# Local attention with channel mix: scores moved behind the attention products, transposes one key block earlier, and a strict order on TensorE

## The chip, the core and the metric

The kernel runs on one core of one Trainium2 chip. The metric is the time of one execution on the device in microseconds (us). A core has five engines that matter here, each with its own instruction queue: TensorE (PE in the profile; its weight loads are listed as PEld), VectorE (DVE), ScalarE (ACT), GpSimd (POOL) and SyncE (SP), which issues the transfers between the chip's memory and the core.

## The reference

Two layers are computed one after the other in float32. The first is attention in chunks of 32 queries, each of which sees the 16 keys to its left, its own 32, 8 to its right and 8 memory keys (64 in all). The second is a channel mix over the 512 joined features, with a hidden width of 1024:

```python
# B, H, S, D = 4, 8, 768, 64; chunk, left, right, n_mem = 32, 16, 8, 8
scores = scale * np.matmul(q_c, k_full.transpose(0, 1, 3, 2))
scores = scores - np.max(scores, axis=-1, keepdims=True)
a = np.exp(scores)
a = a / (np.sum(a, axis=-1, keepdims=True) + 1e-09)
out[:, :, c_start:c_end] = np.matmul(a, v_full)
...
x = np.ascontiguousarray(attn_out.transpose(0, 2, 1, 3)).reshape(B, S, H * D)
x_prev = np.concatenate([np.zeros((B, 1, D), dtype=np.float32), x[:, :-1, :]], axis=1)
xk = mu_k * x + (1.0 - mu_k) * x_prev
xr = mu_r * x + (1.0 - mu_r) * x_prev
k = np.maximum(xk @ w_k, 0.0)
v = k * k @ w_v
r = 1.0 / (1.0 + np.exp(-(xr @ w_r)))
return (r * v).astype(np.float32)
```

## The kernel before

**Units.** The 4 x 768 tokens are cut into 12 units of 256 tokens (NU, UTOK), each of two query tiles of 128 tokens; a batch element has three units. Unit u owns the query tiles 2u and 2u+1. What runs for a unit, in the names that the code and the profile use:

- *Scores* (`scores`, f_s, L429; tile s in PSUM): 128 small matmuls of q with its window of keys, on array tiles of 64 rows by 32 columns. Then the softmax: maximum (L442) and subtraction (L447) on VectorE, exp on ScalarE (L453), sum and reciprocal (L457 to L459) and the normalising product (L463) on VectorE, all in one tile e, of which there is a single buffer, as there is of s.
- *Transposes* (`attention`, f_t, L509; tile pt): eight per unit, four for each query tile, each 128x128. Four copies bring them to SBUF (f_bd; recorded in the helper `copy` at L271 on ScalarE and L273 on VectorE; tile aTz).
- *Attention products* (f_a, L526; tile px): 64 matmuls of aTz with the window of V, on array tiles of 128 rows by 64 columns. Copies bring them to xT (f_x), the channel mix's input.
- *Mixing* (`prep`): difference to the token before (L607), the two mixes (L617), and each split into a high part (xh, L271 or L273) and a low part (xl, L633), since TensorE's matmuls here work on such parts, three matmuls for each product.
- *Gates* (`channel_mix`, f_gate, L951; tile pr): two blocks "g" of 24 matmuls, then the sigmoid on ScalarE (L963; tile sg).
- *Key blocks* "h" (f_s1, L1028; tile ph): four blocks of 24 matmuls, each followed by relu (L1047) and square (L1054, L1056), giving kf.
- *Second projection*: units 0 and 1 do it directly ("v", L1112 and L1124; tile pv). From unit 2 on (FAST = 2) `products` does it with seven products of half-size operands instead of eight. Their operands are sums and differences of quarters of kf (L779, L784), split into high (ah, L271 or L273) and low parts (al, L801). Product n is a block "p" of 12 matmuls (L856) onto one of three PSUM tiles: 1 and 2 onto accx, 7 and 4 onto accz, 6, 5 and 3 onto accy. Between two products on the same PSUM tile VectorE must have read it: f_a0 (a copy), L895 and L898 (additions into the output tile o). At the end come the gate products (L916, L926, L928) and the stores (L901). accx and accz share their two PSUM buffers (tag "tp") with pt and px.

**What sets the order.** The program is a plan. Every step is an operation with an engine or a choice of engines, a cost, dependencies, the buffers it takes and uses, and a due time. `te_order` writes TensorE's order down as a list: LEAD for the start, then a loop over the units. From its list it gives each TensorE operation a due time. For a unit from 3 to 9 the list before is

    h0 h1 | t t (unit u+1) | h2 | a a (unit u+1) | h3 | p1 p7 | s (unit u+2) | g g (unit u+1) | p6 p4 p5 p2 p3

where t are the transposes, a the attention products and s the scores. In unit 10 the transposes stand behind h0 already; there and in unit 11 one of the last unit's two gates fills the middle, and no scores are left (s exists up to unit 11, and stands in the list of unit 9). In unit 11, product 2 is written as two halves with product 3 between them.

`Plan.order` runs the planner three times (TURNS), each with due times from the turn before. In a turn, `Plan.turn` always takes the operation that can start earliest by the model of costs, waits and free buffers (`place`), with later due times as a small handicap (EASE). For TensorE only the first operation of the list is looked at while fewer than STRICT operations are placed, that is in strict order; after that any of the next LOOK = 400 may be taken, so that TensorE need not keep the list:

```python
for o in q[: 1 if e == "pe" and len(done) < STRICT else LOOK]:
```

The engines then execute their own queues in the planned order, with semaphores for the dependencies. An engine waits at the head of its queue; nothing behind overtakes.

Of the kernel before, what the change touches and what calls it, by code (L numbers as in the profile page):

```python
# [25 lines left out]
FT = DFF // P  # L26
# [1 line left out]
NEG = -3.0e38  # L28
TINY = 2.0**-112
LOOK = 400  # L30
STRICT = 230
EASE = 0.1
TURNS = 3
LEAD = "s0.0 s0.1 t0 a0 t1 a1 h0.0.0 h0.0.1 s1.0 h0.1.0 h0.2.0 s1.1 h0.3.0 h0.3.1 h0.3.2 h0.3.3 g0.0 g0.1 t2 t3 v0.0.0 a2 a3 v0.0.1 s2.0 v0.1.0 v0.1.1 h1.0 h1.1 t4 t5 h1.2 a4 a5 h1.3 g1.0 g1.1"
# [1 line left out]
FAST = 2  # L36
# [44 lines left out]
class Plan:  # L81
# [7 lines left out]
    def op(self, alts, fn, deps=(), new=(), use=(), due=1e9):  # L89
        fixed = isinstance(alts, tuple)  # L90
        if fixed:
            alts = [alts]
        o = Op([(a + (False,))[:3] for a in alts], fn, deps, new, use, due)
        o.seq, o.fixed = len(self.ops), fixed
        self.ops.append(o)
        return o
# [53 lines left out]
    def turn(self, goal, ease):  # L150
# [9 lines left out]
        while len(done) < len(self.ops):  # L160
            best = None
            for e, q in todo.items():
                for o in q[: 1 if e == "pe" and len(done) < STRICT else LOOK]:
                    p = self.place(o, free, held)
# [21 lines left out]
def te_order():  # L186

    nu = B * S // UTOK
    seq = [tuple([x[0]] + [int(n) for n in x[1:].split(".")]) for x in LEAD.split()]
    for u in range(1, nu):  # L190
        a, b = 2 * u + 2, 2 * u + 3
        g = [("g", u + 1, c) for c in range(QPU)]
        h = [("h", u, f) for f in range(FT // 2)]
        v = [("v", u, c, n) for c in range(QPU) for n in range(2)]
        n = 1 if u == nu - 2 else 2
        seq += h[:n] + [("t", a), ("t", b)] + h[n : n + 1] + [("a", a), ("a", b)] + h[n + 1 :]
        if u >= FAST:
            v = [("p", u, n) for n in (1, 7, 6, 4, 5, 2, 3)]
            if u >= nu - 2:
                g = [("g", nu - 1, u - (nu - 2))]  # L200
            if u == nu - 1:
                v = v[:5] + [("p", u, 2, 0), ("p", u, 3), ("p", u, 2, 1)]
            seq += v[:2] + [("s", u + 2, 0)] + g + v[2:]
            continue
        seq += v[:1] + [("s", u + 2, 0)] + g + v[1:]
    seq = list(dict.fromkeys(seq))
    last = {"t": B * NQT, "a": B * NQT}
    seq = [x for x in seq if x[1] < last.get(x[0], nu)]
    due, t = {}, 6.0
    for x in seq:  # L210
        assert x not in due
        due[x] = t
        t += PE_COST[x[0]] * (0.66 if x[:3] == ("h", 0, 0) else 0.33 if x[:3] == ("h", 0, KT - 1) else 1.32 if x[:2] == ("h", 0) else 1.32 if x[1] == 0 and x[0] in "gv" else 1)
    return due
# [3 lines left out]
def local_attention__then__channel_mix(  # L218
# [60 lines left out]
    units = [(b, u * UTOK) for b in range(B) for u in range(S // UTOK)]  # L279
    NU = len(units)  # L280
    due = te_order()
    chunks = [(w_k, wk_hl, k) for k in range(KT)]
    chunks += [(w_r, wr_hl, k) for k in range(KT // 2)]
# [93 lines left out]
    def wdeps(hl, ks):  # L377
        return [o for k in ks for o in wdone[id(hl[0]), k]]
# [364 lines left out]
    def products(u, ks, o_g, sgs):  # L743
# [3 lines left out]
        b, t0 = units[u]  # L747
# [98 lines left out]
        def f_p(n, cs):  # L846
            def go():
                name, slot = banks[n]
                if n in fresh:
                    T["acc", u, name] = ps(slot.tag, f"acc{name}{u}")  # L850
                o = pairs(T["acc", u, name][:, : DM // 2])
                for c in cs:
                    xh, xl = T["ah", u, n][:, c], low(n)[:, c]
                    wh, wl = weight_of(n, c)
                    for i, (x, w) in enumerate(((xh, wh), (xh, wl), (xl, wh))):
                        nc.tensor.matmul(  # L856
                            o, x, w, start=(n in fresh and c + i == 0), stop=(c == cs[-1] and i == 2), skip_group_check=True
                        )

            return go  # L860

        def prod(n, deps, cs=range(FT // 2), key=()):
            if n in (1, 2, 3):
                wd = wdeps(wv_hl, [0, 1] if n == 1 else [2, 3])
            else:
                wd = turned[n]
            slot = banks[n][1]
            p[n] = op(
                ("pe", 1.36 * len(cs) / 4), f_p(n, list(cs)), list(parts[n]) + wd + deps,
                new=[slot] if n in fresh else [],  # L870
                use=[hs[n], ls[n][0]] + turn_use + ([] if n in fresh else [slot]),
                due=due[("p", u, n) + key],
            )
            return p[n]
# [44 lines left out]
        if last:  # L919
            p2 = prod(2, [p1, a0], range(FT // 4), (0,))  # L920
            p3 = prod(3, [p5, c22])
            p2 = prod(2, [p2], range(FT // 4, FT // 2), (1,))
        else:
            p2 = prod(2, [p1, a0])
            p3 = prod(3, [p5, c22])
# [9 lines left out]
    def channel_mix(u):  # L935
# [160 lines left out]
        if u >= FAST:  # L1096
            products(u, ks, o_g, sgs)
            return
# [75 lines left out]
    with tc.manual_schedule():  # L1174
        for o in plan.order():
            if o.eng == "pe":
                n = 0 if ("ph", 0, 0) in T else int((o.start - busy - 0.2) / (0.43 if busy else 0.86))
# [56 lines left out]
```

## Time and profile before

| | |
|---|---|
| median of 3 runs | 388.85 us (388.57 to 389.3) |
| the profiled execution | 388.38 us |
| span of its instructions | 386.6 us |
| mean granted TensorE clock | 1.000 |
| bytes moved | 48.98 MB, 127 GB/s on average |
| VectorE busy | 317.6 us, 508 instructions |
| ScalarE busy | 220.4 us, 327 instructions |
| a unit in the steady part (units 3 to 8) | 29.97 us |

The span runs from the first to the last instruction; what remains up to the execution's time is start and end around it. In the page, busy times are per engine, and the slices are fortieths of the span. The chain of waits follows the work that ended last back to the start and prints it in order of time: start, duration, engine, tile and line, and a count. It puts each piece at the end of the one before, so that its times lie up to some 0.2 us behind the starts that the timeline shows. The timeline prints start, duration, engine, line, operation, tiles (output <- inputs), shapes and count; in brackets stands the idle time before the instruction and what ended it. Matmuls are pipelined: each lasts longer than the distance to the next.

### The profile page before, as it was taken

The numbers are of one execution on the slowest core, as the hardware profiler recorded it, in microseconds if no ns is written. First come the engines' busy times: TensorE is split into PE (matmuls) and PEld (weight loads), VectorE is DVE, ScalarE is ACT, GpSimd is POOL, SyncE is SP. The second block draws the span as 40 slices with busy tenths as digits, with TensorE's granted clock in tenths as the row PEclk, the third lists the DMA queues.
The fourth block names the chain that finished last, engine by engine and source line by source line (L and its number), as shares of the span: only waits on it lengthen the run. The fifth ranks groups of instructions, "written<-read, shape, count | busy, mean of one in ns | idle before, by whom it ended". The sixth has DMA issues, their size and how long they took to land.

```text
span 386.6 us, 10715 instructions
## 1 busy us (share of the span) xinstructions
PE 380.0 (98%) x4768; PEld 350.2 (91%) x4768; DVE 317.6 (82%) x508; ACT 220.4 (57%) x327; POOL 2.8 (1%) x13
## 2 busy tenths in 40 slices
PE   8899999999999999999999999999999999999996
PEld 6786549989999999999999999999999999999996
DVE  3989998998799699699699699789779879969264
ACT  1789975662644565464565466376267256567260
POOL 2000000000000000000000000000000000000000
PEclk9999999999999999999999999999999999999999
DMA  8999881221152052143134134134134130000101
GB/s 317 420 407 409 310 297 55 110 83 42 27 204 84 30 177 100 54 136 142 56 116 159 57 110 164 56 109 166 56 110 164 57 100 12 30 29 2 54 2 54
DMA packets 13053, 48.98 MB, mean 127 GB/s; under 512 B 1488, under 2 KB 1872, under 8 KB 12496
## 3 DMA queue, kind: packets, MB, share of 16 engines
q1 hardware_dynamic: 13008, 48.31, 33.5%
q8 instruction: 37, 0.61, 0.7%
q14 instruction: 8, 0.07, 0.1%
HBM read 42.01 MB, written 6.29 MB: 125 GB/s over the span
## 4 chain that ended last, share of the span: by engine, by line
PE 96%; DVE 1%; DMA 1%; issue 0%; ACT 0%
PE ph L1028 31%; PE pr L951 15%; PE accy L856 10%; PE accx L856 7%; PE accz L856 7%; PE px L526 6%; PE s L429 4%; PE ph L1000 4%; PE pv L1112 4%; PE pt L509 3%; PE pv L1124 3%; PE pr L943 2%; DMA qk<-in_qk_dram 1%; PE warm L1180 0%; DVE mx L442 0%
## 5 line engine op out<-in xcount | busy, mean ns | idle before, releaser
L1028 PE MATMUL ph<-xh,wk 128*128 128x256 f32 x352 | 99.0, 281 | 0.0
L1028 PE MATMUL ph<-xl,wk 128*128 128x256 f32 x352 | 96.8, 275 | 0.0
L1028 PE MATMUL ph<-xh,wl 128*128 128x256 f32 x352 | 96.8, 275 | 0.0
L1047 ACT ACTIVATE kf<-ph 128x512 f32<-128x512 f32 x47 | 28.0, 597 | 74.4 <-PE ph L1028 74.3
L1028 PEld LDWEIGHTS ph<-xh,wk 128*128 128x128 f32 x352 | 67.5, 192 | 0.9 <-issue 0.2
L1028 PEld LDWEIGHTS ph<-xl,wk 128*128 128x128 f32 x352 | 67.5, 192 | 0.3 <-issue 0.2
L1028 PEld LDWEIGHTS ph<-xh,wl 128*128 128x128 f32 x352 | 67.6, 192 | 0.0
L273 DVE COPY aTz<-pt 64x512 f32<-64x512 f32 x20 | 13.9, 694 | 28.0 <-PE pt L509 18.0
L951 PE MATMUL pr<-wr,xh 128*128 128x512 f32 x88 | 34.3, 390 | 0.0
L801 DVE TENSOR_TENSOR al<-kf,ah 128x512 fp32r<-128x512 f32 x50 | 33.5, 684 | 0.4
L951 PE MATMUL pr<-wl,xh 128*128 128x512 f32 x88 | 33.4, 379 | 0.0
L951 PE MATMUL pr<-wr,xl 128*128 128x512 f32 x88 | 33.4, 379 | 0.0
L453 ACT ACTIVATE e<-e 128x1024 f32<-128x1024 f32 (+1 forms) x13 | 12.9, 992 | 33.6 <-DVE e L447 33.6
L526 PEld LDWEIGHTS px<-aTz,vw 128*64 128x64 f32 x768 | 23.5, 138 | 3.8 <-issue 2.6
L271 ACT CAST ah<-kf 128x512 fp32r<-128x512 f32 x41 | 25.5, 624 | 1.7 <-DVE kf L779 1.1
L526 PE MATMUL px<-aTz,vw 128*64 128x64 f32 x768 | 25.2, 224 | 1.1 <-issue 1.1
L1054 ACT ACTIVATE kf<-kf 128x512 f32<-128x512 f32 x40 | 25.3, 633 | 1.3 <-DVE kf L1049 0.4
L271 ACT CAST xh<-df 128x1024 fp32r<-128x1024 f32 x11 | 16.4, 1493 | 12.2 <-DVE df L617 12.2
L856 PE MATMUL accx<-wv,ah 128*128 128x256 f32 x80 | 22.0, 275 | 0.0
L856 PE MATMUL accx<-wl,ah 128*128 128x256 f32 x80 | 22.0, 275 | 0.0
L856 PE MATMUL accx<-wv,al 128*128 128x256 f32 x80 | 22.0, 275 | 0.0
L963 ACT ACTIVATE sg<-pr 128x512 f32<-128x512 f32 x24 | 14.3, 605 | 9.8 <-PE pr L951 9.8
(124 smaller groups left out, 934.7 us busy)
## 6 DMA issues: line engine op xcount, KB each, us to landing
qk<-in_qk_dram SPq DMA_DIRECT2D x24, 768.0 KB, 6.0
vw<-in_vw_dram SPq DMA_DIRECT2D x24, 512.0 KB, 4.7
out_dram<-o SPq DMA_DIRECT2D x23, 256.0 KB, 2.0
raw<-in_w_k_dram SPq DMA_DIRECT2D x4, 1024.0 KB, 12.0
raw<-in_w_v_dram SPq DMA_DIRECT2D x4, 1024.0 KB, 8.6
raw<-in_w_r_dram SPq DMA_DIRECT2D x2, 1024.0 KB, 8.1
out_dram<-o SPq DMA_DIRECT2D x2, 128.0 KB, 1.7
id_sb<-in_ident_dram SPq DMA_DIRECT2D x1, 64.0 KB, 5.6
```

Source lines behind the costliest of these rows:

```text
L271: e.copy(dst, src)
L429: nc.tensor.matmul(s5[CHUNK * j : CHUNK * (j + 1), h, d - c, r, :], q4[z, r, j, :], k4[z, r, j, :], start=True, stop=True,)
L526: nc.tensor.matmul(p3[64 * h : 64 * h + 64, 2 * g : 2 * g + 2, CHUNK * j : CHUNK * j + CHUNK], v[:, g, h, j, :], a[:, h, g, j, :], start=True,
L801: nc.vector.tensor_sub(low(n), place[n](), T["ah", u, n].bitcast(F32))
L856: nc.tensor.matmul(o, x, w, start=(n in fresh and c + i == 0), stop=(c == cs[-1] and i == 2), skip_group_check=True)
L951: nc.tensor.matmul(pairs(p), x[:, k, c * P : (c + 1) * P], woven(w), start=(k + n == 0), stop=(k == KT - 1 and n == 2),)
L963: nc.scalar.activation(sg, p, AF.Sigmoid)
L1000: nc.tensor.matmul(p[:, i * UTOK + c * P : i * UTOK + (c + n) * P], T["w", id(wk_hl[0]), k][:, fc], T["xf", u, 0][:, k, z], start=(i + k + ...
L1028: nc.tensor.matmul(pairs(p[:, i * UTOK : (i + 1) * UTOK]), w[:, fc], x[:, :, k].rearrange("p t n -> p n t"), start=(k + n == 0), stop=(k = ...
L1047: e.activation(part(), p, AF.Relu)
L1054: e.activation(q, q, AF.Square)
L1112: nc.tensor.matmul(p, T["kf", u, f // 4][:, f % 4, c * P : (c + 1) * P], w, start=(f == 0), stop=(f == FT - 1))
```

## The change

Three things are edited, all in the order of TensorE's work; no operation is added or removed.

- STRICT goes from 230 to 2000.
- In the list of te_order, for units above FAST the transposes stand behind the first key block instead of the second, the attention products behind the second instead of the third, and the scores of unit u+2 directly behind the attention products of unit u+1 instead of behind p1 p7. Unit 2 keeps its order. For units 3 to 9 the list becomes

      h0 | t t | h1 | a a | s | h2 h3 | p1 p7 | g g | p6 p4 p5 p2 p3

- In the last unit, the second half of product 2 also depends on product 3.

```diff
-STRICT = 230
+STRICT = 2000
...
-        n = 1 if u == nu - 2 else 2
-        seq += h[:n] + [("t", a), ("t", b)] + h[n : n + 1] + [("a", a), ("a", b)] + h[n + 1 :]
+        n = 1 if u > FAST else 2
+        s = [("s", u + 2, 0)]
+        near, far = (s, []) if u > FAST else ([], s)
+        seq += h[:n] + [("t", a), ("t", b)] + h[n : n + 1] + [("a", a), ("a", b)] + near + h[n + 1 :]
         if u >= FAST:
...
-            seq += v[:2] + [("s", u + 2, 0)] + g + v[2:]
+            seq += v[:2] + far + g + v[2:]
             continue
         seq += v[:1] + [("s", u + 2, 0)] + g + v[1:]
...
         if last:
             p2 = prod(2, [p1, a0], range(FT // 4), (0,))
             p3 = prod(3, [p5, c22])
-            p2 = prod(2, [p2], range(FT // 4, FT // 2), (1,))
+            p2 = prod(2, [p2, p3], range(FT // 4, FT // 2), (1,))
```

## Prediction

> **What bounds the kernel now.** I read the page first, then the chain of waits, then the sums per stretch, then the timeline at single joints. The page's head and its first two parts:
>
> ```profile
> span 386.6 us, 10715 instructions
> PE 380.0 (98%) x4768; PEld 350.2 (91%) x4768; DVE 317.6 (82%) x508; ACT 220.4 (57%) x327; POOL 2.8 (1%) x13
> PEclk9999999999999999999999999999999999999999
> ```
>
> TensorE (PE) is busy 98% of the span, and the second row has its granted clock: 9, nine tenths or more, in every slice. The chain, here for unit 6, says in which order it works, and the last row is the sum over that stretch, in busy us of PE, of its weight loads, of VectorE (DVE) and of ScalarE (ACT):
>
> ```profile
> 214.59 5.36 PE ph L1028 x48
> 219.95 0.87 PE pt L509 x8
> 220.82 2.68 PE ph L1028 x24
> 223.50 2.02 PE px L526 x64
> 225.52 2.88 PE ph L1028 x24
> 228.39 1.34 PE accx L856 x12
> 229.73 1.34 PE accz L856 x12
> 231.07 1.42 PE s L429 x89
> 232.49 5.38 PE pr L951 x24
> 237.86 1.34 PE accy L856 x12
> ...
> 214.59:244.56 29.97, 29.97 (x406) 28.92 (x406) 25.25 (x42) 16.41 (x26) 0.00 (x0) 1.00 0.30 107
> ```
>
> A unit takes 29.97 us and PE waits for nobody in it: the reader is to see that each piece begins where the last one ends. So only two things can move the time: what PE itself spends, above all at the joints between unlike blocks, and a wait that a new order brings. DVE has 25.25 of 29.97 us filled and works in a fixed queue; it is the engine that could bring one.
>
> **The joints.** A key block (ph) and a product (acc) issue a matmul every 0.11 us. Here are the attention products (px) entered and left, then the scores (s) entered and left (start, duration, line, count):
>
> ```profile
> 223.23 0.28 PE L1028 MATMUL ph<-xh,wl 128*128 128x256 f32 x1
> 223.43 0.28 PE L526 MATMUL px<-aTz,vw 128*64 128x64 f32 x2
> ...
> 224.76 0.75 PE L526 MATMUL px<-aTz,vw 128*64 128x64 f32 x20
> 225.45 0.38 PE L1028 MATMUL ph<-xh,wk 128*128 128x256 f32 x1
> 225.66 0.28 PE L1028 MATMUL ph<-xl,wk 128*128 128x256 f32 x1
> 225.77 0.28 PE L1028 MATMUL ph<-xh,wl 128*128 128x256 f32 x1
> ...
> 230.80 0.28 PE L856 MATMUL accz<-wv,al 128*128 128x256 f32 x1
> 231.00 0.31 PE L429 MATMUL s<-qk 64*32 64x64 f32 x11
> ...
> 232.42 0.48 PE L951 MATMUL pr<-wr,xh 128*128 128x512 f32 x1
> 232.74 0.38 PE L951 MATMUL pr<-wl,xh 128*128 128x512 f32 x1
> ...
> L526 PE MATMUL px<-aTz,vw x64: 222/222/270, 223.4 to 225.3; 128*64 128x64 f32 x64
> ```
>
> Entering px: 223.43 - 223.23 = 0.20, where 225.77 - 225.66 = 0.11 is the pace, so 0.09 is lost. Leaving px: the last starts at 224.76 + 0.75 - 0.22 = 225.29, the key block at 225.45, 0.16 later; px's own pace is 2.02 / 32 = 0.06 per pair, so 0.10 is lost, and the second key matmul comes 0.21 after the first, another 0.10. Together 0.20. Entering s: 231.00 - 230.80 = 0.20, again 0.09 lost. Leaving s shows its second half in the same way: 0.32 between the first two pr, against a pace of 5.38 / 24 = 0.22.
>
> **Part 1, scores behind the products (units 3 to 9, seven of them; s(12) does not exist, and unit 2 keeps the old place).** Before, a unit enters and leaves px, and enters and leaves s. Afterwards it enters px, goes straight to s, and leaves s. Removed are one leaving of px (0.20) and one entering of s from a full-size block (0.09), 0.29 together; added is one joint px to s, which no row shows. Its bounds: 0.00 if s simply follows at px's pace, 0.29 if it costs what both old joints cost; more has no reason, since at worst PE empties and starts anew, which is what these rows contain. I take 0.10, the first half of leaving px: the last products have to run out, but the second half belongs to a full-size block that must fetch a second set of weights, while the first eleven scores begin within 0.31 - 0.22 = 0.09 us. So 0.29 - 0.10 = 0.19 per unit, times 7 = 1.33 us, bounds 0 and 2.03.
>
> The Trainium skill (TensorEngine Tiling (Array Packing), Key Properties) says that changing the tiling mode, not merely the tile, drains TensorE. The new neighbours have different tiles, 128x64 and 64x32, so by the rule this joint still drains; it denies the end of 2.03 and goes with the 1.33.
>
> Nothing else on PE changes its count: the transposes (pt) stand between two key blocks before and after, the gates (pr) then follow accz, both full size.
>
> **Part 2, what each move does to the waits.** The first row here is from the list of DMA issues (median us from issue to landing last), the second from DVE's timeline:
>
> ```profile
> qk<-in_qk_dram SPq DMA_DIRECT2D x24, 768.0 KB, 6.0
> 232.69 0.68 DVE L801 TENSOR_TENSOR al<-st,ah 128x512 fp32r<-128x512 f32 x1
> ```
>
> By the chain, scores begin 231.07 - 214.59 = 16.5 us into their unit now and will begin where px ends, 225.52 - 214.59 - 2.68 = 8.3 us into it, 8.2 earlier. They need their q and k: loads land in a median of 6.0 us once the scores before have freed the buffer, and scores are a unit of 30 us apart, 30 - 8.2 = 21.8 once, from unit 2 to 3. So that wait isn't near.
>
> SP's queue only gets these loads earlier; they stand ahead of stores and V loads whose owners come later. Products 6 and 4 come 1.42 us nearer to key block 3, as s no longer stands between; the operand al of product 6 is ready at 233.37 and its product stands in the chain at 237.86, so 4.5 us of cover shrink to 3.1: nothing. The gates get 2.68 us more after the products they depend on: nothing lost.
>
> The transposes come 2.68 us earlier, and behind a waiting transpose everything on PE queues up, since PE takes its blocks in order. From unit 4 on their softmax can start 8.2 us earlier and is long done. In unit 3 it isn't: scores 4 are still at the old place.
>
> ```profile
> 123.50 0.68 DVE L916 TENSOR_TENSOR o<-o,sg 128x512 f32<-128x512 f32 x1
> 126.67 0.36 DVE L928 TENSOR_TENSOR o<-o,sg 128x256 f32<-128x256 f32 x1
> 126.95 1.21 DVE L463 TENSOR_TENSOR e<-e,sum 128x1024 f32<-128x1024 f32 x1
> 129.87 0.27 PE L509 MATMUL pt<-id_sb,e 128*128 128x128 f32 x1
> ```
>
> The normalised e is ready at 126.95 + 1.21 = 128.16; the transposes move from 129.87 to 127.19. With DVE's order as it is that is a wait of 1.0 us, once. The planner can put the two gate products of 0.68 and 0.36 behind, 1.04 in all, but then exp on ScalarE, which they cover, lies bare in part. Bounds 0 and 1.0; I take 0.4.
>
> **Part 3, STRICT.** The 508 + 327 + 13 compute instructions of the page, PE's 4768 matmuls in at most some 400 blocks (12 to 128 in a block, but for 24 blocks of 4 transposes) and its 60-odd loads and stores are well under 2000 operations, so the whole list is now kept as written. Up to unit 8 PE keeps it already (the chain). In units 9 to 11 the planner took product 2 ahead of 5 and put product 3 behind the next key block; undoing that costs PE nothing by count. Product 5 must wait for the addition that reads accy after 6, and in unit 6, in the strict order already, this was:
>
> ```profile
> 238.18 1.23 DVE L442 TENSOR_REDUCE mx<-s 128x16 f32<-128x1024 f32 x1
> 239.32 0.41 DVE L898 TENSOR_TENSOR o<-accy,o 128x256 f32<-128x256 f32 x1
> 240.38 0.28 PE L856 MATMUL accy<-t1h,ah 128*128 128x256 f32 x1
> ```
>
> Ready at 239.73, used at 240.38: 0.65 us of cover, taken as 0 cost; without it, the rival below.
>
> **Part 4, the tail.** Half of product 2 now comes last instead of product 3.
>
> ```profile
> 381.61 1.35 PE accy L856 x12
> ...
> 382.98 0.44 DVE o L898
> ...
> 383.44 0.42 DVE o L928
> out_dram<-o SPq DMA_DIRECT2D x2, 128.0 KB, 1.7
> ```
>
> Now two DVE steps hang on PE's end, done at 383.86. Afterwards product 3 ends 0.67 sooner, at 382.29; its two steps run to about 383.19, and product 2's single multiplication (0.42) follows to 383.62. Gain 0.24. If the planner puts that multiplication first, 0.02. The two stores then start 0.4 us apart and may hinder each other, by at most that 0.4. I take 0.2, bounds -0.16 and 0.24.
>
> **The sum.** The profiled run took 388.38 us (span 386.6 and 1.8 around it). -1.33 + 0.4 - 0.2 = -1.13 gives 387.25 for such a run; the median, 388.85, is 0.47 above it, so 387.7 us. That is 0.29% faster; about 0.2%, or 0.78 us, is what a measurement of this kernel can tell from no change.
>
> **Rivals.**
>
> *The joint is free* (s starts at px's pace): 2.03 in place of 1.33, so 387.0. For it: px takes its own tiles in turn without a gap. Against: every shown change of block costs 0.09 or more. Chance 0.08.
>
> *The gain is given back on DVE's additions.* The softmax's steps of 1.2 us now fall elsewhere; where one begins just as product 6 or 5 ends, the addition comes up to 1.2 - 0.65 = 0.55 us too late for product 5 or 3. At 0.16 a unit, 7 x 0.16 = 1.1 us, and the time is 388.8. For it: mx in the row above already holds that addition up. Against: it has cost PE nothing yet. Chance 0.15.
>
> *Slower: the copies between transposes and products.*
>
> ```profile
> 220.42 0.69 DVE L273 COPY aTz<-pt 64x512 f32<-64x512 f32 x1 [2.35 <-PE pt L509]
> ...
> 222.24 0.69 DVE L273 COPY aTz<-pt 64x512 f32<-64x512 f32 x1 [1.13 <-ACT aTz L271]
> ```
>
> With two on ScalarE between those shown they run one after another to 222.93, and px starts at 223.43: 0.50 of cover, and DVE had stood idle for 2.35 us to be there in time. With the transposes a block earlier that idle time is not given. If a step of 1.21 us has just begun, px waits 0.7 us; on average over the chances of meeting one 0.36, times 7 = 2.5, and the time is 387.7 + 2.5 = 390.2. It is slower by over 0.2% once the first copy is late by 0.50 + (1.13 + 0.78) / 7 = 0.77 us in each unit. For it: the backlog ended at 220.42 - 2.35 = 218.07, 3.5 us into the unit, and the first copy could start 220.42 - 214.59 - 2.68 = 3.2 us into it. Against: most of that backlog is softmax, which moves away. Chance 0.15.
>
> *The change does not do what it says*: PE's order stays, because the planner swaps around it. The list is strict and short enough; 0.02, at 388.8.
>
> **How the numbers follow.** The forecast has 0.60: its own range is 388.85 - 2.0 to 388.85 - 0.3, as its stall and its joint fall; I give 0.10 of it to a gain under 0.78. Faster: 0.50 + 0.08, and 0.02 of the give-back case at less than half its price: 0.60. Same: 0.10 + 0.11 + 0.02 = 0.23. Slower: 0.15 and 0.02 of the give-back at its full price: 0.17. The low end is the free joint without a stall in unit 3, 388.85 - 2.03 - 0.2 = 386.6; the high end takes in the give-back with room and the copies at 0.24 a unit, 387.7 + 1.7 = 389.4.
>
> **What would show it.** Right: units 3 to 9 last 29.78 instead of 29.97; s stands 0.15 to 0.16 after the last px; at most one wait on PE before pt, in unit 3; the last DVE step ends about 0.24 nearer to PE's end. Wrong: units at 29.97 (the joint costs 0.29), a wait of px for aTz, of accy for o, or of pt for e in every unit, or a last store that lands later than 1.7 us after its issue.

## The result, and the profile after

| | before | after |
|---|---|---|
| median | 388.97 us (4 runs, 388.57 to 389.3) | 394.0 us (4 runs, 393.43 to 394.48) |
| the profiled execution | 388.38 us, span 386.6 | 394.48 us, span 392.4 |

After over before is 1.0128, 95% interval 1.0116 to 1.0141. The kernel became 5.0 us slower; the prediction was 387.7 us, faster.

From the page of the kernel after, the head, the busy times and the queue of instructions (packets, MB, share of 16 engines):

```profile
span 392.4 us, 10730 instructions
...
PE 380.6 (97%) x4768; PEld 350.6 (89%) x4768; DVE 314.1 (80%) x509; ACT 222.9 (57%) x326; POOL 3.3 (1%) x13
...
q8 instruction: 37, 0.61, 0.6%
```

The work is the same, 4768 matmuls, and the mean granted clock of the profiled execution is 0.998. TensorE's busy time grew by only 0.6 us while the span grew by 5.8, so time was added in which TensorE stood. The view of who waited for whom, TensorE after (total us, times, longest):

```profile
PE ph L1030 <- issue: 3.3, 3, 1.4
PE s L431 <- issue: 2.1, 3, 0.9
...
PE px L528 <- issue: 1.1, 2, 0.6
PE accy L858 <- DVE o L900: 0.4, 1, 0.4
```

Before, the rows with "issue" were these, both from the start of the kernel:

```profile
PE px L526 <- issue: 1.1, 2, 0.6
PE s L429 <- issue: 0.3, 1, 0.3
```

"Issue" is idle time for which the profile shows no releaser. No engine, tile or semaphore is named: no VectorE, no copy, no load. The chain of waits says where this time lies (start, duration, engine, tile, line, count):

```profile
125.26 2.68 PE ph L1030 x24
...
131.50 2.02 PE px L528 x64
133.51 1.41 PE s L431 x89
134.92 1.98 PE ph L1030 x16
136.90 1.27 issue
138.18 3.73 PE ph L1030 x32
...
166.06 0.91 issue
...
195.69 1.10 PE s L431 x72
196.78 0.90 issue
197.68 0.46 PE s L431 x29
...
218.26 2.68 PE ph L1030 x24
...
224.49 2.02 PE px L528 x64
226.51 1.41 PE s L431 x89
227.92 5.55 PE ph L1030 x48
...
287.51 2.87 PE ph L1030 x24
290.39 0.66 issue
...
316.70 1.41 PE s L431 x91
318.11 1.37 issue
...
339.56 2.68 PE ph L1030 x24
```

The reader should look at what stands on each side of an idle row. In unit 3 TensorE stops after 16 matmuls of a key block and goes on with the 17th; in units 4 and 5 it stops in the middle of the scores. A wait for an operand or a buffer is expected at the beginning of a block; these three waits are inside blocks that had already begun. In units 8 and 9 the wait stands just ahead of the first matmul of a key block (behind 24 key matmuls, and behind the scores), so there its place alone doesn't tell it from a wait for data; the count below does. Five of the seven units have one, always in the scores or in the key blocks right behind them; units 6 and 7 have none. The sum over unit 6 and the joint from px to s in unit 3, with the wait behind it:

```profile
218.26:248.03 29.77, 29.77 (x406) 28.85 (x406) 24.56 (x43) 16.95 (x25) 0.00 (x0) 1.00 0.29 107
```

```profile
132.70 0.81 PE L528 MATMUL px<-aTz,vw 128*64 128x64 f32 x22
133.44 0.25 PE L431 MATMUL s<-qk 64*32 64x64 f32 x2
...
136.63 0.28 PE L1030 MATMUL ph<-xh,wk 128*128 128x256 f32 x1
138.18 0.27 PE L1030 MATMUL ph<-xl,wk 128*128 128x256 f32 x1 [1.27 <-issue]
```

The last px starts at 132.70 + 0.81 - 0.22 = 133.29 and the first score at 133.44, 0.15 later, as forecast; a unit without a wait lasts 29.77 instead of 29.97, as forecast. From the first key matmul of unit 3 to that of unit 10 it is 339.56 - 125.26 = 214.30 us, against 7 x 29.97 = 209.79 before: 4.5 more. From one matmul's start to the next, with the ordinary pace taken off, the five waits are 1.44 + 1.09 + 1.08 + 0.83 + 1.44 = 5.88 us (the chain shows less, as a matmul's record lasts 0.28 us and the pace is 0.11). Five waits less the seven joints, 5.88 - 7 x 0.20 = 4.5, is the whole difference of these units.

The row "q8 instruction" of the page leads further. It has 37 packets and 0.61 MB, which is 64 bytes for each of the 2 x 4768 matmuls and weight loads: TensorE's own instruction stream, in blocks of 16 KB, or 256 instructions. Here is each wait by the number of matmuls started before it. Twice that number is the count of matmuls and weight loads; "others" are the further instructions of TensorE that the trace records up to there, its semaphore instructions and one drain at the start. The sum is compared with the next multiple of 256:

```
unit  resumed at  matmuls  x2     others  sum    next border      missing
3     138.18      1748     3496   24      3520   14 x 256 = 3584   64
4     166.97      2128     4256   32      4288   17 x 256 = 4352   64
5     197.68      2508     5016   40      5056   20 x 256 = 5120   64
8     291.05      3776     7552   64      7616   30 x 256 = 7680   64
9     319.48      4156     8312   72      8384   33 x 256 = 8448   64
```

The waits stand a whole number of blocks of 256 apart, to the instruction. What the constant 64 is, the trace doesn't show; 64 instructions at the program's start that it doesn't record would give it. In the experiments below there are 20 more waits on issue of over 0.25 us in units 3 to 9, and all of them stand at 63 or 64 missing. So TensorE stops each time at the border of an instruction block.

The fetch of each of these blocks, from the raw records of the instruction queue (us):

```
unit  fetch starts  takes  TensorE at border  resumes   start to use
3     135.80        0.96   136.63             138.18    2.4
4     164.53        0.88   165.85             166.97    2.4
5     195.05        1.35   196.57             197.68    2.6
6     224.37        0.95   227.14             no wait   (2.8)
7     259.78        0.94   262.97             no wait   (3.2)
8     288.73        0.96   290.11             291.05    2.3
9     316.78        1.09   317.90             319.48    2.7
```

A block is used 2.3 to 2.7 us after its fetch began. In units 6 and 7 TensorE comes to the border 2.8 and 3.2 us after, and does not wait.

### The profile page after: what moved, and what is told of

The parts are those of the page before. It is cut to its first block, busy times and chain, and to the rows that moved or that the text cites. A ratio compares the mean times of both kernels' runs of the same rounds, so it can differ in the third digit from the quotient of the medians.

```text
span 392.4 us, 10730 instructions
## 1 busy us (share of the span) xinstructions
PE 380.6 (97%) x4768; PEld 350.6 (89%) x4768; DVE 314.1 (80%) x509; ACT 222.9 (57%) x326; POOL 3.3 (1%) x13
## 4 chain that ended last, share of the span: by engine, by line
PE 93%; DVE 3%; issue 2%; ACT 1%; DVEq 0%
PE ph L1030 31%; PE pr L953 14%; PE accy L858 10%; PE px L528 6%; PE accz L858 6%; PE accx L858 6%; PE s L431 4%; PE ph L1002 4%; PE pv L1114 4%; PE pt L511 3%; PE pv L1126 3%; PE pr L945 2%; PE warm L1182 2%; DVE al L803 1%; DVE df L619 0%
## 5 line engine op out<-in xcount | busy, mean ns | idle before, releaser
L273 ACT COPY aTz<-pt 64x512 f32<-64x512 f32 x35 | 19.3, 580 | 57.9 <-PE pt L511 56.5
L1049 ACT ACTIVATE kf<-ph 128x512 f32<-128x512 f32 x32 | 19.0, 600 | 36.6 <-PE ph L1030 36.5
L1056 ACT ACTIVATE kf<-kf 128x512 f32<-128x512 f32 x47 | 29.9, 636 | 11.1 <-DVE kf L1051 10.3
L275 DVE COPY aTz<-pt 64x512 f32<-64x512 f32 x13 | 9.0, 693 | 21.4 <-ACT aTz L273 19.7
L275 DVE CAST ah<-kf 128x512 fp32r<-128x512 f32 x16 | 6.8, 427 | 19.3 <-ACT kf L1056 19.0
L273 ACT CAST ah<-kf 128x512 fp32r<-128x512 f32 x34 | 21.1, 624 | 0.9 <-DVE kf L781 0.6
L431 PEld LDWEIGHTS s<-qk 64*32 64x32 f32 x1536 | 16.1, 105 | 5.5 <-issue 4.2
```

The lines of the kernel that those rows point to most:

```text
L273: e.copy(dst, src)
L275: e.tensor_copy(dst, src)
L431: nc.tensor.matmul(s5[CHUNK * j : CHUNK * (j + 1), h, d - c, r, :], q4[z, r, j, :], k4[z, r, j, :], start=True, stop=True,)
L1049: e.activation(part(), p, AF.Relu)
L1056: e.activation(q, q, AF.Square)
```

## The experiments

Three theories stood against each other. The first: attention products and scores back to back use instructions faster than they are fetched. 64 + 128 matmuls with their weight loads are 384 instructions in 2.02 + 1.41 = 3.43 us, 112 in a microsecond, where a key block uses 48 in 2.68 us, 18 in a microsecond. The second: VectorE's new order, the early transposes or the strict list cost the time. The third: the loads of q, k and V, which now start during this stretch, delay the fetch.

**The scores far again, all else as after.**

```diff
-        near, far = (s, []) if u > FAST else ([], s)
+        near, far = [], s
```

> The kernel after, with the scores of every unit back behind products 1 and 7; the transposes stay a key block earlier, STRICT stays at 2000. Theory 1 (instruction supply: products and scores back to back use 192 matmuls in 3.4 us, and the blocks of 256 instructions that TensorE fetches come too late when a block's border falls into the last part of the scores): no wait on issue inside key blocks or scores, units of 29.97 us, some 389 to 389.8 us with the wait before product 3 in unit 10 left. Theory 2 (VectorE's new order, brought by the strict list and the early transposes, makes TensorE wait): still over 392 us. Theory 3 (the loads of q, k and V now start together and hold the instruction fetches up): as theory 1, since the loads come apart again.

Measured: 394.51 us, 1.0139 [1.0123, 1.0154] of the kernel before. TensorE's waits and, from the timeline of unit 3, the addition that the wait names, with a step of the softmax ahead of it:

```profile
PE accy L858 <- DVE o L900: 3.6, 8, 0.6
...
PE s L431 <- issue: 0.3, 1, 0.3
```

```profile
151.92 1.21 DVE L459 TENSOR_REDUCE sum<-e 128x16 f32<-128x1024 f32 x1
...
153.54 0.36 DVE L900 TENSOR_TENSOR o<-accy,o 128x256 f32<-128x256 f32 x1
```

```profile
154.05 0.35 PE L858 MATMUL accy<-wv,ah 128*128 128x256 f32 x1 [0.57 <-DVE o L900]
```

The waits on issue inside the units are gone with the near scores, as the first theory has it. The total, though, is what the second theory would give, and the waits show that it acts as well: product 3 now waits in eight units for the addition that reads accy after product 5. VectorE has a softmax sum of 1.21 us ahead of that addition. A likely reason, not tested by itself, is that transposes moved up with scores left far behind leave the softmax little time. The early transposes have a cost of their own in this place; in the kernel after, the near scores, which start the softmax 8 us earlier, take it away again. So the times of these two kernels are equal by two different causes.

**The near scores alone, on the kernel before, with STRICT at 230.**

```diff
+        s = [("s", u + 2, 0)]
+        near, far = (s, []) if u > FAST else ([], s)
-        seq += h[:n] + [("t", a), ("t", b)] + h[n : n + 1] + [("a", a), ("a", b)] + h[n + 1 :]
+        seq += h[:n] + [("t", a), ("t", b)] + h[n : n + 1] + [("a", a), ("a", b)] + near + h[n + 1 :]
...
-            seq += v[:2] + [("s", u + 2, 0)] + g + v[2:]
+            seq += v[:2] + far + g + v[2:]
```

> The kernel before, with the scores of units 3 to 9 directly behind the attention products and nothing else changed: transposes behind the second key block, STRICT 230, no new dependency. Theory 1: three to five units wait 0.8 to 1.5 us on issue, the other two to four gain 0.19; 391 to 393.5 us. Theory 2: the joint's gain alone, 387.6 us. Theory 3: the loads crowd here too, so all units with a fetch in the crowd wait; 391 to 394 us.

Measured: 393.51 us, 1.0118 [1.0101, 1.0135]. This is not the clean test it was meant to be: after 230 operations the planner is free, and it carried the scores from behind px back, unit by unit, to their old place. The waits on issue came to 3.2 us on the way, two in the middle of the scores (0.99 and 2.23 from start to start), and the additions cost 0.14 to 0.25 in a unit. The waits are there without the early transposes and without the strict list; the total says no more.

**The strict list alone, on the kernel before.**

```diff
-STRICT = 230
+STRICT = 2000
```

> The kernel before, with STRICT at 2000 and nothing else. Units 3 to 8 keep their order, so 29.97 us each and no waits there; what it can cost is a wait of product 3 or 5 for VectorE in units 9 to 11, 0.6 us in the kernel after: 388.9 to 390 us. If the strict list itself spoils VectorE's order: over 391 us.

Measured in 10 runs: 389.97 us, 1.0023 [1.0013, 1.0032]. Its only new row among TensorE's waits is this one, in unit 10:

```profile
PE accy L856 <- DVE o L898: 0.4, 1, 0.4
```

From start to start product 3 loses 0.59 in unit 10 and product 5 loses 0.17 in unit 9, 0.76 together, of the 0.93 us that the medians differ; the second matmul of each comes another 0.07 late. The planner had taken product 2 ahead of 5 there for a reason.

**The near scores and the strict list with the transposes at their old place.**

```diff
-        n = 1 if u > FAST else 2
+        n = 1 if u == nu - 2 else 2
```

> The kernel after, with the transposes back behind the second key block as in the kernel before (scores directly behind the attention products, STRICT 2000). Theory 1: the waits on issue come with the scores' place, whatever the transposes do: units 3, 4, 7, 8 and 9 wait, some 5 to 6 us in all, the joints give 1.36 back, 393 to 394.5 us. If the early transposes were the cause: 388 us.

Measured: 393.45 us, 1.012 [1.0099, 1.0142]. Waits on issue in units 3 (1.36), 4 (0.78), 8 (1.44) and 9 (0.80); unit 7, expected to wait too, did not. The early transposes are not needed for the slowdown.

**The work shifted against the borders.** If the waits are at borders of instruction blocks, a few more instructions at the start must move them to other places of the same units. The warm-up matmuls at the start were cut, first in two and then in four, which adds 32 and 96 matmuls; nothing uses their output.

```diff
-                    nc.tensor.matmul(warm[:, : 2 * P], zero_sb[:, :P], zero_sb, start=True, stop=True)
+                    for z in range(2):
+                        w = slice(z * 2 * P // 2, (z + 1) * 2 * P // 2)
+                        nc.tensor.matmul(warm[:, w], zero_sb[:, :P], zero_sb[:, w], start=True, stop=True)
```

> The kernel after, with each warming matmul at the start cut into two of half the width: 32 more matmuls and 32 more weight loads ahead of everything, in the time in which TensorE waits for the first loads, so that each border between blocks of 256 instructions moves by 32 matmuls against the work. Theory 1: the waits move with the borders. They were in units 3, 4, 5, 8 and 9 with the border at 264, 240, 216, 272 and 248 matmuls into the unit, and none at 192 and 168. Now the borders are at 296, 272, 248, 224, 200, 304 and 280 for units 3 to 9: waits in unit 4 (about 0.8 us), 5 (1.5), 6 (1.1), perhaps 7 and 9 (up to 0.5), none in 3 and 8; 392 to 393.5 us. Theory 2 and theory 3: waits stay in units 3, 4, 5, 8 and 9, 394 us.

Measured: 396.57 us, 1.0187 [1.0172, 1.0202]. From the chain, units 3, 5, 7 and 9:

```profile
134.95 1.04 issue
...
195.05 1.41 PE s L431 x89
...
258.00 1.14 issue
...
318.56 1.35 issue
```

The waits end at matmuls 1748, 3396, 3776 and 4156 of the program, three of them the very counts of the kernel after (and 3396 matmuls with 56 others are 27 x 256 - 64 instructions, a border again), although the work there is now 32 matmuls earlier in its unit. Unit 5 lost its wait and unit 7 got one, with the same order of work and the same loads; unit 4 kept a small one of 0.40. Which way the borders would move was wrong in the expectation: more instructions ahead bring the borders to earlier work. The total, too, lies above the 392 to 393.5 us expected: the waits sum to 6.4 us, 1.90 of them in unit 8, and in the profiled execution 1.3 us more lie behind the last matmul, where the last two stores land 3.1 us after their issue instead of 1.7.

> The kernel after, with each warming matmul cut into four of a quarter of the width: 96 more matmuls and weight loads ahead of everything. In the run with 32 more, the waits came at the 1748th, 3396th, 3776th and 4156th matmul, and three of these numbers were those of the kernel after, so the borders between instruction blocks stand at fixed counts and move towards earlier work when something is put ahead (the expectation of that run had the direction wrong). With 96 more, the borders nearest to the scores of units 3 to 9 are at 168, 271, 247, 223, 199, 176 and 279 matmuls into the unit (and scores run from 120 to 248). Theory 1: waits in units 4 (about 0.8 us), 5 (1.5) and 6 (1.1), little or none in 3, 7, 8 and 9; the waits inside scores and key blocks sum to 3 to 4.5 us. Theory 3: waits stay in the units in which they were in the kernel after.

Measured: 411.85 us, 1.0573 [1.0531, 1.0616], but 15 us of this arise at the start, before the first attention products (28.6 us instead of 13.3), so the total tells nothing and only the units are read. Units 3, 5, 6, 8 and 9 in the chain:

```profile
150.63 1.41 PE s L431 x89
...
211.89 1.54 issue
...
242.98 0.69 issue
...
302.46 1.41 PE s L431 x89
...
332.24 1.41 PE s L431 x91
```

Unit 6, free of waits after, has one, and units 3, 8 and 9 are free. The waits end at matmuls 2636 and 3016, with 40 and 48 others 21 x 256 - 64 and 24 x 256 - 64 instructions. From start to start units 4, 5 and 6 lose 0.26 + 1.61 + 0.88 = 2.75 us, slightly below the 3 to 4.5 expected; unit 4's was to be about 0.8.

**The loads later.** First by the planner: the loads of q, k and V also depend on product 7 (`o.deps.append(p7)`).

> The kernel after, with the loads of q, k (for unit u+3) and V (for unit u+2) held back in units 3 to 9 until product 7 of unit u is issued, so that they no longer run while attention products and scores use instructions fast. Theory 1: the waits stay, 393 to 394.5 us. Theory 3: they vanish, 388 to 389 us. A mixture, which the times of the fetches suggest (in units 3 and 8 the fetch began 2.4 us after its turn while loads ran, in units 4 and 9 at once): units 3 and 8 lose their waits of 1.4 and 0.8 us and unit 5 part of its 1.0, units 4 and 9 keep theirs; 391 to 392 us. Theory 2: 394 us.

Measured: 393.82 us, 1.012 [1.0105, 1.0135]. Inconclusive: this dependency only sets the place in SyncE's queue, and the loads started as early as in the kernel after, 132.5 us in unit 3. So they were held by data: GpSimd copies one element of the unit's output tile into each buffer before its load, in units 3 to 9.

```diff
+    def hold(tile, u):
+        if u > FAST:
+            nc.gpsimd.tensor_copy(tile[0:1, 0:1], T["o", u, 1][0:1, DM // 2 : DM // 2 + 1])
...
+            hold(a, u - 3)
...
+            hold(v, u - 2)
...
+                o.deps.append(ac)
```

> The kernel after, with the loads of q, k and V in units 3 to 9 really held back: GpSimd copies one element of the unit's output tile, written after product 7, into each buffer that is about to be loaded, so that the load must wait for it (the run before only changed their place in SP's queue, and they started at the same times). The loads then run beside the gates, not beside products and scores. Theory 1 pure: waits stay as they are, 394 us. Theory 3: they vanish, 388 to 389 us. Mixture: units 3 and 8, where the fetch started 2.2 to 2.4 us late, lose theirs, units 4 and 9, where it started at once, keep theirs of 1.1 to 1.5 us, unit 5 keeps half: 391 to 392 us.

Measured: 392.06 us, 1.0081 [1.0066, 1.0096]. Units 3 and 4 in the chain:

```profile
133.68 1.41 PE s L438 x89
135.09 5.58 PE ph L1043 x48
...
163.49 1.36 PE s L438 x93
164.85 0.65 issue
```

Units 3 and 8 lost their waits, and 4, 5 and 9 kept theirs (0.83, 1.38, 1.38). This fits the fetches of the kernel after. In units 4, 5, 6 and 9 the fetch starts 110 to 136 matmuls ahead of its border, about one block, and no packet of a load is in flight as it starts; in units 3 and 8 it starts only 8 and 13 matmuls ahead, with 8 and 16 packets of the loads in flight. With the loads held, it starts 41 and 91 matmuls ahead there. So the loads have a part in two of the five waits, and in the other three the block is fetched a block ahead and still comes too late. The loads aren't all that delays a fetch, though: in unit 5 of this run it starts 1.2 us after the border before it was crossed, instead of 0.5, with no load in flight, and the wait there grew from 1.08 to 1.38.

**Room between products and scores.** The scores behind a further key block, all else as after:

```diff
-        seq += h[:n] + [("t", a), ("t", b)] + h[n : n + 1] + [("a", a), ("a", b)] + near + h[n + 1 :]
+        seq += h[:n] + [("t", a), ("t", b)] + h[n : n + 1] + [("a", a), ("a", b)] + h[n + 1 : n + 2] + near + h[n + 2 :]
```

> The kernel after, with the third key block between the attention products and the scores (h0 t t h1 a a h2 s h3 p1 p7 g g ...). The joint px to s is gone, so 1.33 us of gain with it. Theory 1 (it is the two small-tile blocks back to back that use instructions too fast): nearly no wait on issue, since the block ahead of the scores gives the fetch 2.7 us; what remains is product 3's wait of 0.6 in unit 10; 389.5 to 390.5 us. If the mere place of the scores in the first half of the unit, beside the V loads, were enough: waits in units 3, 4, 8 and 9 stay, over 392 us.

Measured: 390.69 us, 1.0042 [1.0027, 1.0058]. One key block more between the two dense pieces takes 3.3 of the 5.0 us back. What is left in TensorE's waits:

```profile
PE s L431 <- issue: 0.7, 2, 0.4
PE accy L858 <- DVE o L900: 0.5, 1, 0.5
```

Unit 3 still has a wait of 0.6 us and lasts 30.62; the other units last 29.97 to 30.08 us again, as the joint that the change had saved is paid again. The time is a little above the 389.5 to 390.5 us expected.

> As the run before in this call, with the loads of q, k and V held back until product 7 of the unit has been read, too. Theory 1 with the loads as a second cause of late fetches: no wait on issue at all, 389.3 to 390.3 us; and the difference to the run without holding is what the loads did to the fetches there.

This joins the key block and the held loads. Measured: 390.65 us, 1.0042 [1.0028, 1.0056].

```profile
PE s L438 <- issue: 0.3, 1, 0.3
```

No wait on issue is left in the units (the 0.3 is that of the start, as before the change). The median is no better than with the key block alone, though 0.8 us of waits are gone (0.6 in unit 3, 0.2 in unit 8) and the profiled span is 1.1 us shorter; the two cannot be told apart by their medians. What remains above the kernel before is the strict list's 0.9 us and units that are not shorter than before.

**A version that keeps the gain.** On the kernel before, near scores only in units 5, 6 and 7, and STRICT 700, so that the end is free again:

```diff
-STRICT = 230
+STRICT = 700
...
+        near, far = (s, []) if u in (5, 6, 7) else ([], s)
```

> The kernel before, with the scores directly behind the attention products in units 5, 6 and 7 alone, and STRICT 700 so that the list holds up to unit 8 and the planner is free in the last three, as before. With the transposes at their old place the scores of these units hold no border of an instruction block in their last part (in the run with the old transposes they were the ones without a wait on issue). Theory 1: up to 3 x 0.19 = 0.57 us less than before, less the waits of 0.07 to 0.22 us for VectorE's additions seen there in units 6 and 7; 388.4 to 389.1 us, no waits on issue.

Measured: 388.71 us in 11 runs against 388.96 in 15, 1.0002 [0.9992, 1.0013]: no difference. No waits on issue in the units; unit 5 lasts 29.78, but units 6 and 7 last 30.01 and 30.05, as products wait 0.07 to 0.16 for VectorE's additions. No version tried is measurably faster than the kernel before.

## Why the prediction was wrong

**The step that failed** is in the part on what bounds the kernel: "So only two things can move the time: what PE itself spends, above all at the joints between unlike blocks, and a wait that a new order brings", and then of VectorE, "it is the engine that could bring one". The list of what TensorE can wait for left out its own instructions. All the waits that it weighed were therefore waits for data: additions, copies, a normalisation. The sum took the scores directly behind the products as a saving alone, when it also put 192 matmuls with 384 instructions, one and a half blocks, into 3.43 us, while a block needs 2.3 to 2.7 us from the start of its fetch to its use. The profile of before could have raised the question: its page has the queue of 0.61 MB of instructions, and its chain has the 64 products and 128 scores with their durations of 2.02 and 1.42 us, though it shows no wait at a border in these units. By the same count of instructions, the tightest border there lies in the scores of unit 7: the fetch starts at 259.13, in the middle of product 1, and the border comes at 262.08, 2.9 us later, so it was in time with little to spare.

Shown are: the place of the waits (block borders, in every run that has them), that they follow the count of instructions and not the work (32 and 96 matmuls more), that they go when the two dense pieces are pulled apart, and that the loads take part in two of five. Not shown is why a fetch starts late while loads are in flight, and once without them, nor what passes between the landing of a block and its use, which is 1.3 to 1.6 us in the five units.

**Point by point.**

- *Joints, -1.33.* Right in mechanism and size: 0.15 us from the last px to the first s against 0.06 of pace, so 0.10 lost, and units 6 and 7 at 29.77 and 29.82. Seven times 0.20 is 1.4 us, and it is in the time; the five waits of 5.88 us lie on top of it.
- *Transposes of unit 3, +0.4.* It was 0. The planner put the gate products behind the normalisation, and the transposes found e ready by 1.4 us (126.38 against 127.78). From VectorE's timeline after:

```profile
125.17 1.21 DVE L465 TENSOR_TENSOR e<-e,sum 128x1024 f32<-128x1024 f32 x1
126.30 0.69 DVE L918 TENSOR_TENSOR o<-o,sg 128x512 f32<-128x512 f32 x1
```

- *STRICT, 0.* Wrong: 0.93 us by the medians of the strict list alone, and in the kernel after product 3 of unit 10 waits 0.61 from start to start. The cover of 0.65 us was read in unit 6 for product 5; the one that had none was product 3 in unit 10, where VectorE took part of the last unit's mixing (xl, 1.35 us) and an operand of its products (al, 0.67) ahead of the addition.
- *Tail, -0.2.* Right in kind. The last three steps of VectorE:

```profile
388.25 0.42 DVE L900 TENSOR_TENSOR o<-accy,o 128x256 f32<-128x256 f32 x1 [1.03 <-PE accy L858]
388.70 0.42 DVE L930 TENSOR_TENSOR o<-o,sg 128x256 f32<-128x256 f32 x1
389.05 0.42 DVE L928 TENSOR_TENSOR o<-accx,sg 128x256 f32<-128x256 f32 x1
```

  Their order is as forecast. VectorE ends 0.59 us after TensorE's last matmul instead of 0.92, a gain of 0.33, but product 3 lost 0.17 by waiting for VectorE in unit 11, so 0.16 stays.
- *The rivals.* Copies: no wait of px for aTz appeared. VectorE's additions: in units 3 to 9 of the kernel after they cost about 0.1 us at most, but in the one with early transposes and far scores they cost 0.36 to 0.74 us in each of eight units, so the mechanism was real and the near scores covered it. The change did what it says.

**The sum by what was measured**, from the first score to the last matmul's end, which grew from 377.82 to 383.29 us, by 5.47: 5.88 of waits at block borders, -1.4 of joints, +0.68 for product 3 in unit 10, and about 0.4 of small waits of products for VectorE in units 2, 4, 7 and 11, together 5.6.

## What to carry to other kernels

When small matmuls are put back to back, count the instructions, weight loads among them, that fall into each microsecond, and compare the time that one fetched block lasts with the time from the start of a fetch to its use; a saved joint of 0.2 us is cheap beside a wait of 0.8 to 1.4 us. Idle time "on issue" inside a block whose operands are all there is the sign, and the count of instructions at which it ends tells whether it is a block's border. Such a wait moves to another place when an instruction is added anywhere ahead, so one order of work can look good or bad by its phase alone, that is, by where in the work the borders fall: the same order lost 5.9, 6.4 and 2.8 us in its units at three phases here. Pulling the dense pieces apart took 3.3 of the 5.0 us back, at the one phase at which it was tried.

## What the runs showed of the hardware

TensorE's instructions came in blocks of 256, about one block ahead of use, and for the five blocks that were late, 2.3 to 2.7 us passed from the start of the fetch to the first instruction used, of which the transfer itself took 0.9 to 1.35 us.

The Trainium skill (Runtime: NRT & Kernel Launch, Instruction fetch mechanics) says that a sequencer's instructions are refilled in 16 KiB blocks, 256 instructions, by a DMA queue of its own while the current ones execute, and that the price of crossing a border is mostly hidden. The blocks agree with this trace, 37 packets of 0.61 MB together; that the crossing is hidden holds here for most key blocks and for the gates, but not in or right behind attention products and scores in a row, where crossings in five of seven units cost 5.88 us.

Fetches of instructions began late where packets of loads were in flight as they were due: in units 3 and 8 only 8 and 13 matmuls ahead of the border, instead of 110 to 136, and with the loads held these two waits were gone. And a change of tiles from 128x64 to 64x32 on the array cost the same 0.10 us as the first half of leaving px for a full-size block.
